# Block 2 of a Strassen-type SwiGLU kernel goes from two levels with streamed weights to one level with weights on chip, and TensorE's order is pinned

## The chip, the core and the metric

The kernel runs on one core of a Trainium2 chip. The core has TensorE (matmuls, written PE; its weight loads are listed as PEld), VectorE (DVE), ScalarE (ACT), GpSimd (POOL) and SyncE (SP), each with a queue of its own. On-chip memory is SBUF, and matmuls write to PSUM. The metric is the time of one execution on the device, in microseconds (us); less is better. All data are float32.

## The reference

The reference computes a normalised linear attention and feeds it into a gated feed-forward network:

```python
# q, k, v: (8 batches, 8 heads, 576 positions, 64)
kv = einsum('bhsd,bhse->bhde', k, v)
out = einsum('bhsd,bhde->bhse', q, kv)
out = out / sqrt(mean(out * out, axis=-1) + 1e-6) * g_norm
x = out.transpose(0, 2, 1, 3).reshape(4608, 512)      # tokens x model
g = x @ w_gate                                        # 512 x 1536
h = g * (1 / (1 + exp(-g))) * (x @ w_val)             # silu(g) * val
result = h @ w_out                                    # 1536 x 512
```

## The kernel before

**Blocks.** The 4608 tokens are cut into nine blocks of 512 (`BLK`). Each block has its attention (class `Att`), an "up" stage that makes h from x (512 to 1536 features, twice), and a "down" stage that makes the output from h. The attention of a coming block is done as a guest inside the stages of the present one: k-v products (a *visit*, line 370), scores (`heads`, line 425), squares, root, scaling, a transposition, and sums of x.

**Levels.** A product of two matrices cut into 2 x 2 quarters can be made from 7 instead of 8 products of quarters (Strassen's scheme in Winograd's form); the price is sums of quarters before and after. *One level* does this once: a unit `j` of class `Up` covers 256 features in 7 products, numbered 1, 5, 6, 2, 7, 4, 3, each of 4 matmuls with 128 x 128 weights and 256 columns (line 647). There are six units. The four base quarters of the weights lie on chip (`wg`, `wv`); three sums of them go into tiles `t`, made on GpSimd (`Up.prepare`). *Two levels* cut each of the 7 again (class `Inner`, 49 products, line 815). Its 49 weight combinations ("leaves") per unit [...]are written once to a DRAM tile `w` (`leaf_steps`, line 988) and read back in pieces of up to 256 KB into the nine `t` tiles (`Stream.pump`, lines 948 to 959).

**Schedule of blocks.** Block 0 goes up plainly, blocks 1 and 2 one after the other, blocks 3 to 8 in three pairs (class `Pair`, with `Joint`, where a matmul takes both blocks' 128 columns, 256 in all). `DEEP` = 2 is the first block with two levels. So before, block 1 is the only one that goes up by one level, and all leaves are made while it runs: from the `t` tiles for products 5, 7 and 4, and from the base quarters in place. The base quarters of the last two units are made in block 1's down stage (`latest`), and their sends are partly left to block 2's down stage (`owed_sends`). Block 2 takes 16 of its 49 leaves from the modified base quarters on chip (`RESIDENT`, `QUARTER`), the others from the stream; its matmuls have 128 columns, since it is alone.

**Memory.** The 97-KiB `arena` holds, for blocks 0 to 2, the weights (0 to 48), x (from 48), inner sums of x (from 62) and h (from 73); for the pairs, two slots each of x, inner sums and h lie over the same bytes. The ring pool `r` has 5 buffers for pieces of results and for the attention's q, squares and scaled x. PSUM pools: `b` 3 banks (the chain of products 1, 6, 7, 4 is summed on one bank and copied out by ScalarE after each), `c` 2 (products 5, 3), `a` 1 (product 2), `m` 2 (visits and scores).

**What sets the order.** The Tile framework places the instructions of all engines by priorities at build time; each engine's order is then fixed. `tc.issue_after` moves a piece behind an instruction; `in_order(engine)` chains an engine's instructions in the order of the program text, which before is used for VectorE in block 2's up stage. `fill` and `then` are dictionaries of guest work, run after a certain unit or product. `chores` (VectorE and ScalarE work) and `sends` (q loads) are lists from which each product pops one step. `ahead` (lines 1295 to 1335) gives block 2's up stage its guests: attention of block 3, of which x is turned by TensorE transposes (line 485), and k-v visits of block 4. In later blocks x is turned by VectorE in 32 x 32 tiles (`blocks_x`, line 495) and then placed by 16 DMAs (`place_x`, line 508), eight each on the queues of SP and ScalarE.

Of the kernel before, what the change touches and what calls it, by code (L numbers as in the profile page):

```python
# [14 lines left out]
P = 128  # L15
# [3 lines left out]
def kernel(  # L19
# [86 lines left out]
    KIB = 256  # L106
# [14 lines left out]
    SLOT = X + XI_  # L121
    x_slots = [x_of(span(SLOT * i, X)) for i in range(2)]
    xi_slots = [xi_of(span(SLOT * i + X, XI_)) for i in range(2)]
    h_slots = [h_of(span(2 * SLOT + H_ * i, H_)) for i in range(2)]
    both = span(0, 2 * SLOT).rearrange("p (b y) -> p b y", b=2)
    x_both = both[:, :, 0 : X * KIB].rearrange("p b (o k t) -> p b o k t", o=7, k=2)
    xi_both = both[:, :, X * KIB :].rearrange("p b (a l c) -> p b a l c", a=3, l=7)
    h_both = span(2 * SLOT, 2 * H_).rearrange("p (b f t) -> p b f t", b=2, f=NF)
# [103 lines left out]
    class Att:  # L232
# [257 lines left out]
        def blocks_x(self):  # L490


            turned = self.sq.rearrange("p f t j d -> p (f t j d)").rearrange("p (i x) -> p i x", i=2)
            for i in range(2):
                nc.vector.transpose(
                    out=turned[:, i].rearrange("p (j t c) -> p t j c", t=2, c=P),
                    in_=self.xts[:, i].rearrange("p t j u d -> p t j (u d)"),
                )
            self.turned = turned
# [122 lines left out]
    DEEP = 2  # L622
# [46 lines left out]
    class Up(Quad):  # L669
# [51 lines left out]
        def multiply(self, p):  # L721
            super().multiply(p)
            ffn = self.ffn
            if ffn.n != DEEP - 1:
                return

            if p == 5:
                self.leaf_room = ring().rearrange("p f (s c) -> p (f s) c", c=P)
            if p in (5, 7, 4):
                at = 3 * (5, 7, 4).index(p)  # L730
                ffn.making.extend(leaf_steps(self.j, [(self.w[p].unsqueeze(1), (p,))], self.leaf_room[:, at:]))
            if p == 3:
                if ffn.leaf_room is None:
                    ffn.leaf_room = xi_alone.rearrange("p a b c -> p (a b) c")
                halves = lambda t: t[self.j].rearrange("p (o i) c -> p o i c", o=2)
                steps = lambda room: leaf_steps(self.j, [(halves(wg), (1, 2)), (halves(wv), (6, 3))], room)
                if self.j < NP - 2:
                    ffn.later.extend(steps(ffn.leaf_room))
                else:
                    ffn.latest.append(steps)  # L740

    class Inner:
# [12 lines left out]
        def __init__(self, ffn, d, g, shared):  # L755
            self.ffn, self.d, self.g, self.shared = ffn, d, g, shared
            self.outers = self.GROUPS[g]
            self.ps = {}
# [27 lines left out]
        def weight(self, o, p, f):  # L786
            j = 2 * self.d + f
            if o in RESIDENT and p in QUARTER:
                w, r = {1: (wg, 0), 2: (wg, 2), 6: (wv, 0), 3: (wv, 2)}[o]
                i, e = QUARTER[p]  # L790
                return w[j][:, r + i, P * e : P * (e + 1)]
            return stream.use(self.ffn.n, self.d, o, p, f)

        def targets(self, ps, o, p):

            return [(ps[:, f], self.weight(o, p, f)) for f in range(2)]

        def operand(self, o, p):
            x = XO[o]
            if p in XI:  # L800
                return self.ffn.att.xi[:, XI[p], x]
            i, q = {1: (0, 0), 2: (1, 0), 6: (0, 1), 4: (1, 1)}[p]
            return self.ffn.att.x[:, x, i, P * q : P * (q + 1)]

        def multiply(self, p):
# [6 lines left out]
            begins = first  # L812
            for i, o in enumerate(self.outers):
                for to, weight in self.targets(ps[:, i], o, p):
                    self.ffn.multiplied = nc.tensor.matmul(  # L815
                        to, lhsT=weight, rhs=self.operand(o, p), start=begins, stop=True, skip_group_check=True,
                    )
                    begins = False
# [30 lines left out]
        def made3(self, p, e, q):  # L849
            if p != 4:  # L850
                return
            h = self.ffn.h[:, 4 * self.d : 4 * self.d + 4]
            c11, c12, c21, c22 = (self.whole(*i) for i in ((1, 1), (3, 1), (3, 0), (1, 0)))

            engine = nc.gpsimd if 4 * self.d + 4 < NF else nc.vector
            mul(engine, h[:, :, 0:HB], c11, c12)
            nc.scalar.activation(out=c21, in_=c21, func=ACT.Silu)
            mul(engine, h[:, :, HB:BLK], c21, c22)
            self.ffn.ended = self.ffn.h_sums(2 * self.d, 2, engine)

    class Joint(Inner):

        def targets(self, ps, o, p):

            return [(ps, stream.use(self.ffn.n, self.d, o, p))]

        def operand(self, o, p):  # L870
            x = XO[o]
            if p in XI:
                return xi_both[:, :, XI[p], x]
            i, q = {1: (0, 0), 2: (1, 0), 6: (0, 1), 4: (1, 1)}[p]
            return x_both[:, :, x, i, P * q : P * (q + 1)]

        def made3(self, p, e, q):
            if p != 4:
                return
            h = h_both[:, :, 2 * self.d : 2 * self.d + 2]  # L880
# [3 lines left out]
            engine = nc.gpsimd if self.d + 1 < NP else nc.vector  # L884
# [3 lines left out]
            self.ffn.ended = self.ffn.a.h_sums(self.d, 1, engine)  # L888

# [578 lines left out]
```

## Time and profile before

| | us |
|---|---|
| median of 3 runs | 1026.76 (1025.21 to 1027.19) |
| the profiled execution | 1028.97 |
| its span, first to last instruction | 1027.2 |
| start and block 0 up | 114.5 |
| block 0 down | 41.6 |
| block 1 up | 76.6 |
| block 1 down | 38.6 |
| block 2 up | 95.9 |
| block 2 down | 38.8 |
| pairs, up / down | 131 / 77, 130 / 77, 130 / 76 |

The stages are stretches of the span, cut where TensorE goes from one to the next; a few matmuls lie across each cut. A matmul of float32 shows as two records in the profile. A row of groups gives the line, engine, operation, written and read tiles, shapes and count, then busy time and the mean of one, then idle time of the engine before them with what ended it. A row of the timeline gives start, length, engine, line and operation, count, and in brackets the idle time before it. Records of the queues (PEq, SPq, ACTq) are DMA issues or the engine's own control.

### The profile page before, as it was taken

How to read it: one execution, taken by the hardware profiler on the slowest of the kernel's cores; microseconds unless marked ns; L12 is line 12 of the kernel's file. 1: busy time of each engine (PE TensorE's matmuls, PEld its weight loads, DVE VectorE, ACT ScalarE, POOL GpSimd, SP SyncE). 2: the span in 40 equal slices, each digit the busy share in tenths (PEclk: the TensorE clock that was granted, in tenths of full speed). 3: DMA queues.
4: the chain of work that ended last, by engine and by line, in shares of the span. 5: the costliest groups of instructions: out<-in, count | busy, mean ns of one | idle time of the engine just before them, and what ended most of it. 6: DMA issues, size and time to landing. Idle time of an engine off the chain costs nothing.

```text
span 1027.2 us, 17734 instructions
## 1 busy us (share of the span) xinstructions
PE 998.6 (97%) x6774; PEld 839.1 (82%) x6774; DVE 682.8 (66%) x1166; ACT 228.8 (22%) x357; POOL 359.2 (35%) x283
## 2 busy tenths in 40 slices
PE   5999999999989999999999999999999999999998
PEld 4544688888978888888888888888888888888887
DVE  2999688988557597666666755667776566666211
ACT  2765111221111211111211212211112112121100
POOL 0000263434023531444565102555651025556600
PEclk9999999999999999999999999999999999999999
DMA  7689643669788566586752364667412545543011
GB/s 219 198 266 260 122 94 129 215 212 235 230 204 223 147 201 147 164 227 157 168 149 52 101 144 149 162 169 178 120 16 67 134 144 156 161 142 101 1 41 41
DMA packets 255637, 155.20 MB, mean 151 GB/s; under 512 B 141632, under 2 KB 234816, under 8 KB 255552
## 3 DMA queue, kind: packets, MB, share of 16 engines
q1 hardware_dynamic: 215104, 148.95, 52.4%
q10 hardware_dynamic: 40384, 5.12, 3.2%
q8 instruction: 54, 0.88, 0.4%
q14 instruction: 31, 0.25, 0.1%
q0 software_dynamic: 64, 0.00, 0.0%
HBM read 117.97 MB, written 28.70 MB: 143 GB/s over the span
## 4 chain that ended last, share of the span: by engine, by line
PE 69%; DVE 3%; DMA 3%; ACTq 1%; issue 1%; ACT 0%; SPq 0%; DVEq 0%
PE b L815 24%; PE b L647 15%; PE c L815 12%; PE c L647 7%; PE a L815 6%; PE a L647 4%; DMA t<-w 3%; PE m L425 1%; PE m L370 1%; ACTq L508 1%; DVE r L132 1%; DMA ld<-in_k_dram 0%; DVE z L439 0%; DVE arena L133 0%; DVE r L134 0%
## 5 line engine op out<-in xcount | busy, mean ns | idle before, releaser
L815 PE MATMUL b<-arena,t 128*128 128x256 f32 (+1 forms) x1248 | 280.8, 363 | 7.4 <-DMA t<-w 5.3
L815 PEld LDWEIGHTS b<-arena,t 128*128 128x128 f32 x1248 | 221.2, 191 | 39.6 <-DVE r L132 5.3
L132 DVE TENSOR_TENSOR r<-b,r 128x512 f32<-128x512 f32 (+1 forms) x273 | 162.1, 606 | 94.0 <-PE b L815 85.6
L132 POOL TENSOR_TENSOR r<-r 128x256 f32<-128x256 f32 (+1 forms) x105 | 110.7, 1055 | 310.2 <-DMA t<-w 147.4
L132 DVE TENSOR_TENSOR r<-c,r 128x512 f32<-128x512 f32 (+1 forms) x179 | 108.7, 617 | 90.6 <-PE c L815 41.2
L815 PE MATMUL c<-arena,t 128*128 128x256 f32 (+1 forms) x624 | 140.8, 361 | 2.2 <-DMA t<-w 0.8
L133 POOL TENSOR_TENSOR t<-wo 128x512 f32<-128x512 f32 x54 | 76.9, 1447 | 175.8 <-DVE wo L132 105.8
L134 POOL TENSOR_TENSOR arena<-r 128x1024 f32<-128x1024 f32 (+1 forms) x46 | 96.2, 2108 | 90.8 <-DVE r L132 79.7
L815 PEld LDWEIGHTS c<-arena,t 128*128 128x128 f32 x624 | 111.1, 191 | 16.9 <-PE b L815 1.4
L132 DVE TENSOR_TENSOR r<-a,r 128x512 f32<-128x512 f32 (+1 forms) x99 | 62.4, 631 | 91.9 <-PE a L647 58.8
L133 DVE TENSOR_TENSOR arena<-arena 128x512 f32<-128x512 f32 (+3 forms) x101 | 100.5, 1007 | 18.5 <-PE b L647 11.9
L647 PE MATMUL b<-wo,arena 128*128 128x256 f32 x432 | 99.4, 382 | 0.9 <-POOL arena L134 0.8
L647 PE MATMUL b<-t,arena 128*128 128x256 f32 x432 | 96.4, 380 | 1.5 <-ACT r L1075 1.5
L647 PEld LDWEIGHTS b<-t,arena 128*128 128x128 f32 x432 | 81.8, 190 | 13.4 <-issue 2.1
L647 PEld LDWEIGHTS b<-wo,arena 128*128 128x128 f32 x432 | 80.8, 190 | 13.2 <-POOL arena L134 1.2
L829 ACT COPY r<-b 128x512 f32<-128x512 f32 x63 | 36.9, 586 | 226.1 <-PE b L815 209.3
L815 PE MATMUL a<-arena,t 128*128 128x256 f32 (+1 forms) x288 | 72.2, 366 | 0.0
L815 PEld LDWEIGHTS a<-arena,t 128*128 128x128 f32 x288 | 52.9, 190 | 6.6
L647 PE MATMUL c<-t,s 128*128 128x256 f32 x216 | 48.5, 379 | 0.0
L647 PE MATMUL a<-wo,arena 128*128 128x256 f32 x216 | 48.4, 379 | 0.0
L647 PE MATMUL c<-wo,arena 128*128 128x256 f32 x216 | 48.1, 379 | 0.0
L647 PEld LDWEIGHTS a<-wo,arena 128*128 128x128 f32 x216 | 41.0, 190 | 5.6
(118 smaller groups left out, 1115.4 us busy)
## 6 DMA issues: line engine op xcount, KB each, us to landing
t<-w SPq DMA_DIRECT2D x219, 256.0 KB, 3.1
t<-w SPq DMA_DIRECT2D x75, 128.0 KB, 3.1
out_dram<-r SPq DMA_DIRECT2D x17, 512.0 KB, 3.0
ld<-in_k_dram SPq DMA_DIRECT2D x26, 288.0 KB, 4.6
ld<-in_v_dram SPq DMA_DIRECT2D x26, 288.0 KB, 6.5
ld<-in_moe_w_gate_dram SPq DMA_DIRECT2D x12, 512.0 KB, 4.9
ld<-in_moe_w_val_dram SPq DMA_DIRECT2D x12, 512.0 KB, 4.6
ld<-in_moe_w_out_dram SPq DMA_DIRECT2D x12, 512.0 KB, 5.2
```

The costliest lines, as they stand in the source:

```text
L132: add = lambda e, o, a, b: e.tensor_tensor(out=o, in0=a, in1=b, op=OP.add)
L133: sub = lambda e, o, a, b: e.tensor_tensor(out=o, in0=a, in1=b, op=OP.subtract)
L134: mul = lambda e, o, a, b: e.tensor_tensor(out=o, in0=a, in1=b, op=OP.mult)
L370: self.positions = nc.tensor.matmul(self.kv_ps[r][u * D : (u + 1) * D, g, :], lhsT=k[:, u, c, :], rhs=v[:, u, c, :], start=(c == 0), stop= ...
L425: self.multiplied = nc.tensor.matmul(self.ps[i][u][p : p + D, t, j, :], lhsT=self.qt[rows, 2 * i + t, j, p : p + D], rhs=kvs[b % 3][rows, ...
L508: placed = queue.dma_start(out=dst[rows[b], :, rows[a]], in_=src[rows[a], :, rows[b]])
L647: self.ffn.multiplied = nc.tensor.matmul(banks[e][:, e], lhsT=lhsT, rhs=rhs, start=first and i == 0 and (e == 0 or banks[0] is not banks[1 ...
L815: self.ffn.multiplied = nc.tensor.matmul(to, lhsT=weight, rhs=self.operand(o, p), start=begins, stop=True, skip_group_check=True,)
L829: nc.scalar.copy(out=dst, in_=ps)
```

## The change

1. Block 2 goes up by one level, like block 1, from the weights on chip: `DEEP` becomes 3 (`PAIRED`), `Inner` takes over what `Joint` did, and the code for a two-level block alone, with its stream pieces (`ALONE`), goes.
2. The leaves of the base quarters are made in block 2's up stage, in place, after each unit's last product (two steps to a product); in block 1 only those of the `t` tiles are made. The last unit's are made in block 2's down stage, after product 5. No sends are owed.
3. Block 3's attention, a guest in block 2's up stage, uses ring buffers instead of homes in the arena, is turned by VectorE and placed by DMA (`turn_steps`, `place_x`, `gain_x`) instead of by TensorE transposes. Guests are placed by unit and product; each product pops up to two chores and five q loads. The q loads of blocks 3 and 4 in this stage are all issued on SP; before, SP and ScalarE shared them.
4. Block 3's inner sums run after product 7 of block 2's down stage instead of 5; block 2 needs none.
5. TensorE's order is pinned to the program's over all of block 2, and over both down stages of each pair.
6. The pairs' slots in the arena are laid out anew: two x, two inner sums, two h.

```diff
-    SLOT = X + XI_
-    x_slots = [x_of(span(SLOT * i, X)) for i in range(2)]
-    xi_slots = [xi_of(span(SLOT * i + X, XI_)) for i in range(2)]
-    h_slots = [h_of(span(2 * SLOT + H_ * i, H_)) for i in range(2)]
+    x_slots = [x_of(span(X * i, X)) for i in range(2)]
+    xi_slots = [xi_of(span(2 * X + XI_ * i, XI_)) for i in range(2)]
+    h_slots = [h_of(span(49 + H_ * i, H_)) for i in range(2)]
...
         def blocks_x(self):
+            for step in self.turn_steps():
+                step()
+
+        def turn_steps(self):
             turned = self.sq.rearrange("p f t j d -> p (f t j d)").rearrange("p (i x) -> p i x", i=2)
+            self.turned = turned
             for i in range(2):
-                nc.vector.transpose(
+                yield lambda i=i: nc.vector.transpose(
                     out=turned[:, i].rearrange("p (j t c) -> p t j c", t=2, c=P),
                     in_=self.xts[:, i].rearrange("p t j u d -> p t j (u d)"),
                 )
...
-    DEEP = 2
+    DEEP = PAIRED
...
             super().multiply(p)
             ffn = self.ffn
+            if ffn.n == 1:
+                if p == 5:
+                    self.leaf_room = ring().rearrange("p f (s c) -> p (f s) c", c=P)
+                if p in (5, 7, 4):
+                    at = 3 * (5, 7, 4).index(p)
+                    ffn.making.extend(leaf_steps(self.j, [(self.w[p].unsqueeze(1), (p,))], self.leaf_room[:, at:]))
+            if ffn.n == 2 and p == 3:
+                room = xi_alone.rearrange("p a b c -> p (a b) c")
                 halves = lambda t: t[self.j].rearrange("p (o i) c -> p o i c", o=2)
+                steps = leaf_steps(self.j, [(halves(wg), (1, 2)), (halves(wv), (6, 3))], room)
+                if self.j < NP - 1:
+                    ffn.making.extend(steps)
                 else:
-                    ffn.latest.append(steps)
+                    ffn.latest.extend(steps)
...
             for i, o in enumerate(self.outers):
-                for to, weight in self.targets(ps[:, i], o, p):
...
+                self.ffn.multiplied = nc.tensor.matmul(
+                    ps[:, i], lhsT=stream.use(self.ffn.n, self.j, o, p), rhs=self.operand(o, p),
+                    start=first and i == 0, stop=True, skip_group_check=True,
+                )
...
-            base = lambda t=t, os=os: send(os, (1, 6, 2, 3), t.rearrange("p o i e c -> p o (i e c)"))
-            if os[0] in RESIDENT and j >= NP - 2:
-                owed_sends.append(base)
-            else:
-                yield base
+            yield lambda t=t, os=os: send(os, (1, 6, 2, 3), t.rearrange("p o i e c -> p o (i e c)"))
...
-            units = []
-            for d in range(NP // 2):
-                if self.n < DEEP:
-                    units += [Up(self, 2 * d), Up(self, 2 * d + 1)]
-                else:
-                    shared = {}
-                    units += [Inner(self, d, g, shared) for g in range(4)]
+            units = [Up(self, j) for j in range(NP)]
...
-                        self.make(4)
-                        if self.chores:
-                            self.chores.pop(0)()
-                        if self.sends:
-                            self.sends.pop(0)()
+                        self.make(4 if self.n == 1 else 2)
+                        for steps, most in ((self.chores, 2), (self.sends, 5)):
+                            for _ in range(min(most, len(steps))):
+                                steps.pop(0)()
+                    fill.get((i, p) if unit is this else None, lambda: None)()
...
-                if p in (5, 7) and self.n == DEEP - 1:
+                if p == 5 and self.latest:
                     with tc.issue_after(nxt.scaled.ins), tc.issue_after(nxt.placed.ins):
-                        room = self.leaf_room if p == 5 else ring().rearrange("p f (s c) -> p (f s) c", c=P)
-                        for step in self.latest.pop(0)(room):
+                        for step in self.latest:
                             step()
...
-        def load(att, i, *pairs):
-            ffn.sends += att.quarter_steps(i, pairs, (nc.sync, nc.scalar))
+        def load(att):
+            for i in range(2):
+                ffn.sends += att.quarter_steps(i, (0, 1), (nc.sync,))
         def visits():
             visit(ffn, att, (0, 1))
-            load(att, 0, 0, 1)
-            load(att, 1, 0, 1)
+            load(att)
             then.load_kv(0)
         def turn():
             visit(ffn, then, (0,), True)
-            then.load_kv(1)
-            ffn.chores += [lambda i=i: att.turn_q(i) for i in range(2)]
+            ffn.chores += [lambda: att.turn_q(0), lambda: att.turn_q(1), lambda: then.load_kv(1)]
         def half(i):
             with tc.issue_after(ffn.multiplied.ins):
                 att.heads(i, range(NS), (m_psum, m_psum))
             ffn.visited = att.multiplied
             ffn.chores += att.chores(i)
-
-        def turn_x(i):
...
+            if i:
+                ffn.chores += att.turn_steps()
-        att.homes = {
-            "qt": h_alone[:, 8:12], "sq": span(0, 8).rearrange("p (f t) -> p f t", f=4),
-            "xts": span(8, 8).rearrange("p (f t) -> p f t", f=4),
+        return {
+            (0, 7): visits, (1, 7): turn, (2, 5): lambda: (half(0), load(then)), (3, 5): lambda: half(1), (3, 7): last,
+            (4, 5): att.place_x, (5, 1): att.gain_x, (5, 5): lambda: ffn.chores.extend(att.sum_steps()),
         }
...
-        if n:
-            ffn.down_.opens = n + 1
+        if n == 2:
+            ffn.down_.opens = PAIRED
...
-        ffn.down(nxt, {1: send, 5: inner_sums} if n == 2 else {})
+        ffn.down(nxt, {7: inner_sums} if n == 2 else {})
...
+    for n in range(PAIRED):
+        with in_order(nc.tensor.engine) if n == 2 else ExitStack():
+            alone(n)
...
-        pair.a.down(after[0] if after else None, {5: pair.second_sums})
...
-        pair.b.down(after[1] if after else None)
+        with in_order(nc.tensor.engine):
+            pair.a.down(after[0] if after else None, {5: pair.second_sums})
+            if after:
+                after[1].turn()
+            if len(after) > 2:
+                after[2].load_kv(1)
+            pair.b.down(after[1] if after else None)
```

## The prediction

> **What bounds the kernel now.** I read the page's busy times first, then busy time by stage, then TensorE's timeline in the stage that the change rewrites, then the queues of SyncE and ScalarE.
>
> ```profile
> PE 998.6 (97%) x6774; PEld 839.1 (82%) x6774; DVE 682.8 (66%) x1166; ACT 228.8 (22%) x357; POOL 359.2 (35%) x283
> ```
>
> TensorE is the bound, so time is won only where it waits or has fewer columns to do. The stages (window, its length, then busy time of PE, PEld, DVE, ACT, POOL) are block 1 up, block 1 down, block 2 up, block 2 down:
>
> ```profile
> 156.10:232.70 76.60, 76.60 (x486) 66.51 (x485) 65.80 (x134) 17.83 (x32) 30.13 (x23) 1.00 0.59 194
> 232.70:271.30 38.60, 37.84 (x293) 32.91 (x292) 27.72 (x52) 6.49 (x10) 11.36 (x8) 1.00 0.94 245
> 271.30:367.20 95.90, 86.53 (x1039) 81.29 (x1037) 61.04 (x114) 18.12 (x31) 33.92 (x26) 0.98 0.75 186
> 367.20:406.00 38.80, 37.13 (x287) 31.67 (x286) 32.23 (x44) 7.60 (x11) 9.89 (x7) 1.00 0.68 180
> ```
>
> Block 1, one level from weights on chip, needs 76.6 us; block 2, two levels and streamed, needs 95.9 us. TensorE's timeline (start, us, group) gives both paces, a streamed wait, and the pairs' start:
>
> ```profile
> 195.55 1.89 PE L647 MATMUL c<-arena 128*128 128x256 f32 x8
> 197.27 1.89 PE L647 MATMUL b<-arena 128*128 128x256 f32 x8
> ...
> 271.37 0.61 PE L815 MATMUL b<-arena 128*128 128x128 f32 x4
> 271.81 0.61 PE L815 MATMUL b<-arena,t 128*128 128x128 f32 x4
> ...
> 291.55 0.68 PE L815 MATMUL b<-arena,t 128*128 128x128 f32 x4 [1.81 <-DMA t<-w]
> ...
> 405.00 1.03 PE L815 MATMUL b<-arena,t 128*128 128x256 f32 x4
> ```
>
> A product of one level is 4 matmuls or 8 records: 1.725 us. A 128-column record takes 0.445/4 = 0.111 us. Block 2 lasts 405.00 - 271.37 = 133.6 us: 588 small records 65.4, guests in the up stage 4.7 (L370) + 2.2 (L425) + 1.9 (transposes L485), down stage 84 matmuls x 0.4314 = 36.2 and scores of block 4 2.3. That is 112.7; 20.9 us are waits and restarts, about 18 of them in the up stage.
>
> The other facts, from the timelines of SP and ACT, are that 8 q loads take 3.9 us of SP (20.3 for 32 at the worst), and that 8 placing DMAs hold ScalarE for 7.8 us, with a PSUM copy behind them:
>
> ```profile
> 100.09 20.31 SPq L333 DMA_DIRECT2D ld<-in_q_dram  x32
> ...
> 513.53 3.93 SPq L333 DMA_DIRECT2D ld<-in_q_dram  x8
> ```
>
> ```profile
> 386.03 7.76 ACTq L508 DMA_DIRECT2D arena<-r  x8
> 393.84 0.59 ACT L1075 COPY r<-b 128x512 f32<-128x512 f32 x1 [13.99 <-DMA arena<-r]
> ```
>
> [...]leaf subtractions of 128x256 average 0.618 us beside a busy GpSimd, the sums of h of that size 0.421.[...]
>
> **The change part by part.** Times U count from block 2's first product, in the instruction order of the changed program.
>
> *Products.* 42 products x 1.725 = 72.5 in place of 65.4: +7.1. The 16 TensorE transposes go: -1.9. Guests stay: L370 4.6, L425 2.2. All stream waits go: -20.9, against the new waits below. Five interruptions cost about 1.0 of restarts (block 1 up: 76.6 - 72.5 - two visits of 1.2 - 0.9 of down work begun early = 0.8 for two; both ends 0.8 to 2).
>
> *Wait A: q of block 3.* All 32 q loads now sit on SP, behind four k/v loads that wait for their buffers: 5 products 8.6 + half a visit 1.2 = U+9.8; four issues at 0.63 make 12.3. The program gives DMAs eight semaphores in turn, so each waits for the eighth before it; v lands after 6.5 us, which holds two q loads some 2.3. 32 x 0.49 + two leaf sends 1.0 + 2.3 ends at 31.4; landing 2.9 makes 34.3. VectorE, held to written order, is done with its earlier work at about 26.1, turns the first half of q and waits at the second to 34.3, then 1.2: 35.5. Behind it stand, start to start, leaf steps 0.5 + 1.0 + 0.7 + 0.5, two sums of squares 1.2, two PSUM adds 1.2, the root 2.5 (eleven small operations), two scales 1.2: 8.8, to 44.3. TensorE gets to the second half of the scores after 21 products 36.2 + visits 3.4 + first scores 1.1 = 40.7, and both "m" buffers are held until that scale. Its order is pinned, so the k-v visit, all later products and with them every PSUM copy stand behind it: A = 3.6. With q 3 us sooner 0.6; with the slow pace of 0.63 a load, 8.
>
> *Wait B.* From that scale VectorE has, in order: adds 3 x 0.6, h sums 0.7, leaf steps 2.2 + 1.0 + 0.7 + 0.5, sums of squares 1.2, root 2.5, scales 1.2, together 11.8, up to the scale of the other half. TensorE needs 1.1 + 5 x 1.725 = 9.7 to block 4's second k-v visit, which wants the same buffers: B = 2.1. If GpSimd collides less with VectorE, 0; if more, 4.
>
> *Wait C.* Block 3's x is now turned on VectorE, ready 4.7 after that scale (add 0.6, sums 0.7, leaf 1.0, two transposes 2.4), and placed by 8 DMAs on ScalarE and 8 on SP while products run. ScalarE is held 5.6 to 7.8, then Silu 0.6 and the copy that product 7 of unit 4 waits for 0.6: 11.5 to 13.7 after the scale. TensorE is there after 1.15 + 6 x 1.725 = 11.5. C = 0 to 2.2; I take 0.8. The gain by ScalarE waits for landing, with four products of slack: 0.
>
> *Leaf steps of the base blocks.* 12 a unit, 5.2 us of VectorE (2 x (0.618 + 0.577 + 0.799 + 0.618)), beside 2.9 of adds and h sums: 8.1 of a 12.1 us unit; their waits are in A to C. Block 1 is rid of them: it ran 115.3 for 113.3 of work, so 0 to -1.5; I take 0.
>
> *GpSimd.* In its new order 13 subtractions of t (1.43 each), up to unit 4's first, stand ahead of unit 0's h products, and the last two wait for TensorE to free a t tile at U+14.4 and U+16.1. So those products end at 16.1 + 2 x 1.4 + 2 x 1.4 = 21.7, before the h sums at 23.7: 0. Without that cover VectorE would stop there for some 2 us.
>
> *Down of block 2.* The last unit's leaf steps (4.6 of VectorE) and four sends (3.8 of SP) come after block 4's transposes at down+20, its placing to 27.5: sends to about 31, the first stream tiles land by 37 of 39. Hidden; uncovered 1 to 3. The placing still holds ScalarE just past product 4: 0.7 instead of 2.8. The inner sums one product later end before the pair: 0. The new buffers change addresses only: 0.
>
> *Pinned downs of the pairs.* In the first two pairs three filler matmuls go back behind, where nothing waited: 0. In the last pair the filler covers the copy between products 6 and 7:
>
> ```profile
> 961.54 5.34 PE L647 MATMUL b<-wo,arena 128*128 128x256 f32 x24
> 966.72 1.03 PE L647 MATMUL a<-wo,arena 128*128 128x256 f32 x4
> 967.61 5.42 PE L647 MATMUL b<-t,arena 128*128 128x256 f32 x24
> ```
>
> Without it TensorE waits 0.75 to 0.87, twice: +1.7.
>
> *Sum.* Block 2: 72.5 + 6.8 + 1.0 + A 3.6 + B 2.1 + C 0.8 + down 36.2 + 2.3 + 0.7 = 126.0, against 133.6: -7.6; with +1.7, -5.9. The profiled execution took 1028.97 (span 1027.2 and 1.8 around it), 2.2 above the median, so about 1023 for its like and 1026.76 - 5.9 = 1021 for the median.
>
> **Rivals.** *The whole gain comes through:* A, B and C stay small since q lands sooner or the leaf steps run at their uncontended 0.42. Then block 2 is 119 to 121 and the time about 1026.8 - 13 = 1014. For it: block 1 up ran gapless with VectorE busy 65.8 of 76.6. Against it: block 1 had no attention in that stage. *Waits change places:* A + B + C reach 12 to 14 and eat the gain, 1024.7 to 1028.8, near 1027. For it: VectorE's units 2 and 3 carry 8.1 + 5.8 us of work in 12.1. *Slower through SP's queue:* at the 0.63 a q load of the 100 us row, block 3's batch comes 4.5 later (A) and block 4's batch of 32 another 4.5, which delays the leaf sends behind it; their one staging buffer then stops VectorE before B. That is +9, so +3, 1030. It decides once the queue's delay passes 5.9 us, that is above about 0.58 a load. Against it: most rows run at 0.49.
>
> **How the numbers follow.** The measurement tells 0.2% (2.1 us) from no change. Likeliest case, 1017 to 1024.7 (point 1021): 0.50. Whole gain, below 1017: 0.22. Waits change places: 0.12. SP's queue, above 1028.8: 0.16. Faster 0.72, same 0.12, slower 0.16. The range 1013 to 1029 leaves out some 0.05 below (all waits at their lower ends and block 1 faster) and 0.15 above.
>
> **What would show it.** Right: block 2 from first product to the pairs' first in about 126 us; no L815 waits on "DMA t<-w" there; a wait of VectorE's q transpose on the q load near U+27; TensorE stopped before the second scores and the second k-v visit, by VectorE; two waits of 0.8 on ScalarE's copy in the last pair. Wrong: the up stage under 82 us or over 92, a gap before the first pair for stream tiles, or a change in the pair stages (131, 77, 130, 77, 130 us now), which I hold untouched.

## The result, and the profile after

The changed kernel takes 1033.32 us (median of 4 runs, 1031.70 to 1033.66), the kernel before, beside it, 1026.63. The ratio is 1.0064 with a 95% interval of 1.0047 to 1.0082: slower by 6.7 us, where the prediction said 5.9 us faster. The profiled execution took 1033.40, its span 1031.6.

TensorE's busy time on the page hardly moved (998.6 before), while VectorE lost 30 us of work:

```profile
PE 1000.9 (97%) x6506; PEld 835.1 (81%) x6506; DVE 653.2 (63%) x1118; ACT 232.5 (23%) x367; POOL 366.0 (35%) x290
```

The stages are the place to look. The rows are block 1 up, block 1 down, block 2 up and block 2 down; the third number from the end is the granted TensorE clock:

```profile
155.93:232.30 76.37, 76.37 (x486) 66.67 (x485) 45.21 (x105) 17.75 (x32) 28.91 (x23) 1.00 0.50 151
232.30:269.88 37.58, 37.58 (x293) 33.00 (x292) 20.55 (x32) 6.60 (x10) 22.80 (x17) 1.00 0.29 62
269.88:368.99 99.11, 86.01 (x754) 73.44 (x753) 58.75 (x105) 22.79 (x42) 30.10 (x23) 0.93 0.58 152
368.99:407.47 38.48, 38.48 (x298) 33.79 (x296) 33.85 (x52) 6.60 (x10) 10.57 (x8) 1.00 0.80 206
```

Block 1 is 1.3 us shorter (from its first product to block 2's: 113.95, before 115.21), block 2's down stage runs without a wait, and what block 2 loses against the forecast lies in its up stage: 99.1 us, where the terms of the forecast add up to 86.8. It has 13.1 us without a busy TensorE, and a granted clock of 0.93. TensorE's timeline shows both:

```profile
269.88 1.89 PE L650 MATMUL b<-arena 128*128 128x256 f32 x8
...
298.63 0.46 PE L423 MATMUL m<-kv,r 64*64 64x64 f32 x16 [0.55 <-DVE r L384]
306.50 1.56 PE L423 MATMUL m<-kv,r 64*64 64x64 f32 x48 [7.41 <-DVE r L384]
307.99 3.00 PE L650 MATMUL b<-arena,t 128*128 128x256 f32 x8
...
321.28 1.16 PE L423 MATMUL m<-kv,r 64*64 64x64 f32 x64
...
334.98 2.78 PE L368 MATMUL m<-ld 64*64 64x64 f32 x72 [3.71 <-issue]
337.69 3.50 PE L650 MATMUL b<-arena 128*128 128x256 f32 x8
...
350.11 1.97 PE L650 MATMUL b<-arena,t 128*128 128x256 f32 x8 [0.28 <-ACT r L670]
...
364.93 1.96 PE L650 MATMUL b<-arena,t 128*128 128x256 f32 x8 [0.77 <-ACT r L700]
367.15 1.99 PE L650 MATMUL c<-arena 128*128 128x256 f32 x8 [0.26 <-DVE r L130]
...
407.47 1.03 PE L801 MATMUL b<-arena,t 128*128 128x256 f32 x4
```

Two things are seen here. The stage stops twice for long: 0.55 + 7.41 us at the first scores (line 423), and 3.71 us at block 4's second k-v visit (line 368). The row names no engine for the second stop; the visit needs the two PSUM buffers "m" that VectorE's two scales of half 1 free one after the other, and VectorE does these at just that time:

```profile
334.19 1.28 DVE L132 TENSOR_TENSOR r<-m,y 128x512 f32<-128x512 f32 x2
```

What comes right after each stop is slow: a product that takes 1.89 us as listed takes 3.00 and 3.50, the scores 1.56 instead of 0.93 (as in the run with the visits first, below), the visit 2.78 instead of 1.28. That is 1.74 us after the first stop and 3.11 after the second, 4.85 in all. The granted clock of the same stretches:

```profile
305.00:310.00 5.00, 3.50 (x53) 3.02 (x54) 2.76 (x4) 1.08 (x2) 0.00 (x0) 0.50 0.86 255
...
335.00:340.00 5.00, 4.88 (x78) 4.15 (x79) 4.86 (x9) 0.39 (x2) 0.00 (x0) 0.50 0.23 82
```

It falls to 0.50. If the stop is what does this, which is tested below, a stop of TensorE is paid twice here. A stretch at 0.50 is called a dip in what follows; the two here last from 303.24 to 310.06 us and from 333.96 to 340.78.

The first stop goes back to q. VectorE's timeline has the two q transposes, SyncE's the q loads, with a leaf send left out at each row of dots:

```profile
297.25 1.24 DVE L384 STREAM_TRANSPOSE r<-ld 128x1024 f32<-128x1024 f32 x1
305.20 1.25 DVE L384 STREAM_TRANSPOSE r<-ld 128x1024 f32<-128x1024 f32 x1 [6.72 <-DMA ld<-in_q_dram]
```

```profile
283.48 11.97 SPq L331 DMA_DIRECT2D ld<-in_q_dram  x20
...
296.00 3.27 SPq L331 DMA_DIRECT2D ld<-in_q_dram  x5
...
299.79 3.59 SPq L331 DMA_DIRECT2D ld<-in_q_dram  x7
```

The 32 q loads end at 303.38, VectorE turns the second half at 305.20, and TensorE, which came to the first scores at 298.1, goes on at 306.5.

The books of the spans: start and block 0 -0.2, block 1 -1.26, block 2 +3.96 (137.59 from its first product to the pair's, before 133.63), pairs up to the last down stage 0.0, the last pair's down stages +1.9 (77.93, before 76.02). Together +4.4, the difference of the spans (1031.6 - 1027.2). The medians differ by 6.7, because the profiled execution before lay 2.3 us above its median and the one after lies on it; in which stage these 2.3 us lie, no trace shows.

### The profile page after: what moved, and what is told of

Same layout as the page of the kernel before. It is cut to its first block, busy times and chain, and to the rows that moved or that the text cites. A ratio compares the mean times of both kernels' runs of the same rounds, so it can differ in the third digit from the quotient of the medians.

```text
span 1031.6 us, 17068 instructions
## 1 busy us (share of the span) xinstructions
PE 1000.9 (97%) x6506; PEld 835.1 (81%) x6506; DVE 653.2 (63%) x1118; ACT 232.5 (23%) x367; POOL 366.0 (35%) x290
## 4 chain that ended last, share of the span: by engine, by line
PE 90%; DMA 3%; DVE 2%; SPq 2%; ACT 1%; issue 1%; POOL 1%; ACTq 0%; DVEq 0%; POOLq 0%
PE b L650 24%; PE b L801 21%; PE c L650 11%; PE c L801 11%; PE a L650 6%; PE a L801 5%; PE b L1110 4%; PE c L1110 4%; PE m L423 2%; PE m L368 1%; SPq L331 1%; DMA arena<-in_v_dram 1%; POOL t L131 1%; DMA arena<-r 1%; DMA ld<-in_v_dram 1%
## 5 line engine op out<-in xcount | busy, mean ns | idle before, releaser
L801 PE MATMUL b<-arena,t 128*128 128x256 f32 x1008 | 244.5, 381 | 0.0
L801 PEld LDWEIGHTS b<-arena,t 128*128 128x128 f32 x1008 | 190.0, 190 | 29.6 <-DVE r L130 2.4
L130 POOL TENSOR_TENSOR r<-r 128x256 f32<-128x256 f32 (+1 forms) x90 | 94.7, 1053 | 247.1 <-DMA t<-w 150.1
L130 DVE TENSOR_TENSOR r<-b,r 128x512 f32<-128x512 f32 (+1 forms) x234 | 139.0, 607 | 60.8 <-PE b L801 55.4
L132 POOL TENSOR_TENSOR arena<-r 128x1024 f32<-128x1024 f32 (+1 forms) x54 | 102.0, 1904 | 108.1 <-DVE r L130 64.2
L130 DVE TENSOR_TENSOR r<-a,r 128x512 f32<-128x512 f32 x93 | 59.3, 638 | 122.9 <-PE a L650 87.4
L801 PE MATMUL c<-arena,t 128*128 128x256 f32 x504 | 122.5, 379 | 0.8 <-ACT r L815 0.8
L801 PEld LDWEIGHTS c<-arena,t 128*128 128x128 f32 x504 | 95.6, 190 | 14.5 <-ACT r L815 1.2
L131 POOL TENSOR_TENSOR t<-arena 128x512 f32<-128x512 f32 x36 | 48.8, 1366 | 68.6 <-PE b L650 26.4
L801 PE MATMUL a<-arena,t 128*128 128x256 f32 x252 | 66.1, 379 | 0.0
```

The lines of the kernel that those rows point to most:

```text
L130: add = lambda e, o, a, b: e.tensor_tensor(out=o, in0=a, in1=b, op=OP.add)
L131: sub = lambda e, o, a, b: e.tensor_tensor(out=o, in0=a, in1=b, op=OP.subtract)
L132: mul = lambda e, o, a, b: e.tensor_tensor(out=o, in0=a, in1=b, op=OP.mult)
L801: self.ffn.multiplied = nc.tensor.matmul(ps[:, i], lhsT=stream.use(self.ffn.n, self.j, o, p), rhs=self.operand(o, p), start=first and i == ...
```

## The experiments

All are the changed kernel with the edit shown, timed beside the kernel before. "Block 2" is the time from its first product to the pair's first, from the run's trace; it is the sharper measure, since block 1 takes 113.95 or 113.96 us in all the traces of the changed kernel and its variants compared so.

| run | median, us | ratio to before (95%) | block 2, us |
|---|---|---|---|
| before | 1026.63 | 1 | 133.6 |
| after | 1033.32 | 1.0064 (1.0047 to 1.0082) | 137.6 |
| q loads on two queues | 1033.56 | 1.0055 (1.0033 to 1.0077) | 138.1 |
| visit later | 1033.76 | 1.0061 (1.0040 to 1.0082) | 138.9 |
| pairs' order free | 1030.37 | 1.0034 (1.0025 to 1.0043) | 137.3 |
| block 2's order free | 1038.94 | 1.0107 (1.0081 to 1.0134) | 145.0 |
| k-v visits first | 1023.59 | 0.9972 (0.9960 to 0.9983) | 128.2 |
| gap filled | 1031.89 | 1.0052 (1.0035 to 1.0069) | 134.5 |
| attention steps first | 1030.08 | 1.0031 (1.0019 to 1.0042) | 135.6 |
| three edits | 1018.74 | 0.9922 (0.9907 to 0.9937) | 125.7 |
| three + room in turns | 1018.66 | 0.9906 (0.9890 to 0.9922) | 125.6 |
| three + block 4's q later | 1017.92 | 0.9899 (0.9883 to 0.9916) | 124.0 |
| three + both | 1017.34 | 0.9892 (0.9874 to 0.9910) | 123.3 |

The kernel before had medians of 1026.86, 1026.39 and 1028.33 beside the three batches of experiments (the first four edits, the next four, the last three), so between batches the ratios are to be compared, not the medians.

### Undo SyncE's sole load of q

```diff
-                ffn.sends += att.quarter_steps(i, (0, 1), (nc.sync,))
+                ffn.sends += att.quarter_steps(i, (0, 1), (nc.sync, nc.scalar))
```

> The q loads of blocks 3 and 4 in block 2's up stage alternate again between SP and ScalarE; nothing else differs from the changed kernel. Theory 1 (the 32 loads on SP alone make q late, and TensorE's first scores wait for the second q transpose: 0.55 + 7.41 us, then products at a lower granted clock, some 1.7 us more): the first scores wait at most 1.5 us, the dip of the clock behind that wait goes, and the time is about 1025 (1023 to 1027). The wait at the second k-v visit (3.7 us) stays. Rival 2 (VectorE's own backlog makes the transpose late, the queue is only beside it): the wait stays above 5 us and the time within 1031 to 1034. Rival 3 (the loads hold ScalarE, whose copies are then late): the first wait goes but TensorE waits for ScalarE in units 1 and 2 instead, 1029 or more.

The time does not change. TensorE's timeline, then ScalarE's:

```profile
292.33 1.96 PE L650 MATMUL b<-arena,t 128*128 128x256 f32 x8 [1.74 <-ACT r L670]
...
303.67 0.46 PE L423 MATMUL m<-kv,r 64*64 64x64 f32 x16 [4.51 <-DVE r L384]
...
306.19 3.78 PE L650 MATMUL b<-arena,t 128*128 128x256 f32 x8
```

```profile
291.77 5.55 ACTq L331 DMA_DIRECT2D ld<-in_q_dram  x5
297.36 0.59 ACT L700 COPY r<-b 128x512 f32<-128x512 f32 x1 [5.17 <-DMA ld<-in_q_dram]
```

Theory 1 missed by over 8 us. In its numbers the result is the second case (the wait stays above 5 us, the time within 1031 to 1034), in its cause a good part of the third: five loads hold ScalarE for 5.55 us, 1.11 each, so the PSUM copies behind them are late. The copy of line 700 ends 5 us later than in the changed kernel (counted from block 2's first product), VectorE's next addition waits for it (5.63 us), and both q transposes stand behind that addition: they begin at 302.28. The wait at the first scores is still 5.1 us, and 1.74 us are lost before it. Sharing the loads again thus brings nothing back in this order of the program; what SyncE's sole load costs by itself is not shown.

### Move the second k-v visit alone

```diff
-            (0, 7): visits, (1, 7): turn, (2, 5): lambda: (half(0), load(then)), (3, 5): lambda: half(1), (3, 7): last,
-            (4, 5): att.place_x, (5, 1): att.gain_x, (5, 5): lambda: ffn.chores.extend(att.sum_steps()),
+            (0, 7): visits, (1, 7): turn, (2, 5): lambda: (half(0), load(then)), (3, 5): lambda: half(1),
+            (4, 5): lambda: (last(), att.place_x()), (5, 1): att.gain_x, (5, 5): lambda: ffn.chores.extend(att.sum_steps()),
```

> Block 4's second k-v visit moves from after product 7 of unit 3 to after product 5 of unit 4, three products later. Theory 1 (waits stand one behind the other): the 3.71 us wait before the visit goes and with it the slowed products behind it (3.1 us), but TensorE then comes 6.8 us sooner to product 7 of unit 4, whose copy stands behind the placing DMAs on ScalarE; that wait grows from 0.28 to about 6 to 7 us, and the time stays within 1030 to 1034. Rival 2 (the visit's wait alone holds the stage, ScalarE's hold is covered): the stage is 4 to 7 us shorter and the time 1026 to 1029.

As theory 1 had it, with a smaller new wait than its 6 to 7 us. The visit's wait falls to 0.5 us and its dip goes, but TensorE then meets ScalarE's hold by the placing DMAs, which the wait had covered. TensorE, then ScalarE:

```profile
348.19 3.59 PE L650 MATMUL b<-arena,t 128*128 128x256 f32 x8 [5.02 <-ACT r L670]
```

```profile
340.69 6.23 ACTq L511 DMA_DIRECT2D arena<-r  x6
...
347.47 0.58 ACT L670 COPY r<-b 128x512 f32<-128x512 f32 x1
```

The 0.28 us at this copy in the changed kernel becomes 5.02, with a dip of its own (3.59 instead of 1.89; the mean granted clock of the run is 0.993, as in the changed kernel). The waits of this stage lie one behind the other: to take this one away gained nothing (1033.76), since the next is as long.

### The pins on TensorE's order

```diff
-        with in_order(nc.tensor.engine):
+        with ExitStack():
             pair.a.down(after[0] if after else None, {5: pair.second_sums})
```

> TensorE's order is left to the scheduler again in the down stages of the pairs; block 2 stays pinned. Theory: only the last pair changes, where fillers cover the copy between products 6 and 7 again; its two waits of 0.72 and 0.68 us go, and the time is 1.4 to 1.8 us below the changed kernel, about 1031.6. Rival: the pin costs nothing there because the end of the kernel waits for the stores; no change, 1033.3.

The median is 2.9 us below the changed kernel's. The last pair's down stages take 76.2 us instead of 77.9; so 1.7 us are the pin, as the theory had it. The rest is not the edit's as far as the traces show: the one other stretch that differs by over 0.4 us ends where block 1 begins (154.54 against 155.93), ahead of all that the edit touches. The two waits of the changed kernel, and the filler in their place in this run:

```profile
970.10 2.18 PE L650 MATMUL b<-t,arena 128*128 128x256 f32 x9 [0.72 <-POOL s L130]
...
1007.27 5.45 PE L650 MATMUL b<-t,arena 128*128 128x256 f32 x24 [0.68 <-ACT r L670]
```

```profile
962.03 5.34 PE L650 MATMUL b<-wo,arena 128*128 128x256 f32 x24
967.21 1.03 PE L650 MATMUL a<-wo,arena 128*128 128x256 f32 x4
```

The other pin, over block 2, was undone in a run of its own:

```diff
-        with in_order(nc.tensor.engine) if n == 2 else ExitStack():
-            alone(n)
+        alone(n)
```

> TensorE's order is left to the scheduler in block 2; the pairs stay pinned. It then puts the first scores' larger part five products later and the second k-v visit several products later. Theory 1 (the waits come from the places at which the order is pinned): the wait at the first scores falls from 8.0 to 0 to 2 us, and the time is about 1025 (1022 to 1028), not lower because ScalarE's hold by the placing DMAs waits behind. Rival 2 (VectorE's and SP's chains set the end of the stage, whatever TensorE's order): 1031 to 1034. Rival 3 (the granted clock dips at these times by itself, whatever waits come before): the waits go, the dips to 0.5 at some 307 and 337 us of the span stay, about 1028.

All three cases missed: it is 5.6 us slower than the changed kernel. The scheduler does put products ahead of the scores, and the wait there falls to 1.39 us. But VectorE, whose order stays pinned, stops 8.90 us in front of its second q transpose, and after it has the sums, the root and the additions of several products to catch up. TensorE now runs ahead into a full PSUM bank:

```profile
318.47 2.93 PE L650 MATMUL a<-arena 128*128 128x256 f32 x6 [5.63 <-DVE r L130]
```

Later waits of 1.43, 3.71 and 2.44 us follow. The dips now begin at 316.8 and 371.4 us, with the waits of 5.63 and 3.71, and not at some 307 and 337 us, which speaks against the third case. The pin of block 2 is not the cause; with q late, it is the better of the two orders.

### Let q start sooner

```diff
-            (0, 7): visits, (1, 7): turn, ...
+            (0, 1): visits, (1, 7): turn, ...
```

Block 3's k-v visits, whose end frees the buffers for q, come after product 1 of unit 0 instead of product 7.

> Block 3's k-v visits move from after product 7 of unit 0 to after its product 1, so that the buffers for q come free 6.9 us sooner; the loads stay on SP alone. Theory 1 (q is late because its loads start late[...]; ScalarE must not carry them): q lands some 6.9 us sooner, the wait at the first scores falls from 8.0 to 0 to 1.5 us, too short to bring the granted clock down, so its 1.7 us of slowed products go too; the later waits (3.7 us and the second dip) stay. About 1024 (1022 to 1027). Rival 2 (the time comes back at the k-v visit and at ScalarE's hold, because VectorE's chain is no earlier): 1029 or more. Rival 3 (k and v of block 3 are not there yet): a new wait after product 1 of unit 0.

Theory 1 holds, and this one number turns the change from 0.64% slower to 0.28% faster. The k and v of block 3 were there, so no new wait came up. SyncE, then TensorE:

```profile
276.25 17.43 SPq L331 DMA_DIRECT2D ld<-in_q_dram  x32
```

```profile
298.58 0.46 PE L423 MATMUL m<-kv,r 64*64 64x64 f32 x16 [0.56 <-DVE r L384]
299.61 0.93 PE L423 MATMUL m<-kv,r 64*64 64x64 f32 x48 [0.57 <-DVE r L384]
...
326.45 0.33 PE L368 MATMUL m<-ld 64*64 64x64 f32 x4 [3.70 <-issue]
327.05 2.19 PE L368 MATMUL m<-ld 64*64 64x64 f32 x68 [0.27 <-DVE r L132]
```

The loads end 9.7 us sooner, 7.2 by their earlier start and 2.5 because no leaf sends stand among them and one takes 0.545 us instead of 0.59. The wait at the scores is 1.1 us, and nothing after it is slow. Block 2 is 9.35 us shorter: 6.8 of the wait, 1.7 of the first dip, 0.9 of the second, which came out shorter. The 3.70 us at the visit stay, as expected, and the rest of the visit is listed here as waiting for VectorE's scale (line 132).

### Is it the stop that slows what follows?

```diff
         def half(i):
             with tc.issue_after(ffn.multiplied.ins):
+                if i == 0:
+                    spare = m_psum.tile([P, 2, NS, D], F32, name="m").rearrange("p t j d -> p (t j d)")
+                    for _ in range(16):
+                        nc.tensor.matmul(spare[:, 0:256], lhsT=ident, rhs=ffn.att.x[:, 0, 0], start=True, stop=True)
                 att.heads(i, range(NS), (m_psum, m_psum))
```

> 16 matmuls of 128 x 256 columns, whose result nothing reads, stand ahead of the first scores and fill 6.9 us of the wait there; the wait's end is unchanged. Theory 1 (the granted clock falls because TensorE stood still[...]): no dip after the first scores, the product behind them takes 1.73 us instead of 2.84, and the stage is 1 to 2.5 us shorter there; a dip behind the later wait of 3.7 us stays. About 1031.5. Rival 2 (the dip comes from something else that happens at that time, as load on the chip): the dip stays and the time is 1033 or, with the matmuls themselves slowed, up to 1037.

The dip is gone where the gap is filled, and is still there behind the gap that is not. TensorE's timeline, then the windows with the granted clock:

```profile
298.37 7.07 PE L1229 MATMUL m<-arena,ident 128*128 128x256 f32 x32
305.37 0.58 PE L423 MATMUL m<-kv,r 64*64 64x64 f32 x16
306.34 0.93 PE L423 MATMUL m<-kv,r 64*64 64x64 f32 x48 [0.38 <-DVE r L384]
307.19 1.99 PE L650 MATMUL b<-arena,t 128*128 128x256 f32 x8
```

```profile
305.00:310.00 5.00, 4.62 (x80) 3.77 (x79) 2.83 (x4) 1.68 (x3) 0.73 (x1) 1.00 0.72 222
...
335.00:340.00 5.00, 5.00 (x30) 4.17 (x24) 4.08 (x7) 0.98 (x3) 0.00 (x0) 0.71 0.01 3
```

With seven microseconds of useless matmuls, block 2 is 3.1 us shorter. Of these only 1.6 are the filling's: the scores and the product at full pace. A q that came sooner gave 0.6, and a second dip that was shorter 0.8. The medians, 1031.89 and 1033.32, are too close for their intervals to part.

The same holds over all the traces, from some 20 us on, where their clock records begin. A single unfilled wait of TensorE between 2.79 us (room in turns) and 10.45 us (attention steps first) brought a clock of 0.50 each time. Single waits of 1.2 to 2.44 us did not: in the kernel before, the clock is 1.00 through a wait of 1.81 us that ends at 291.55. But two waits close together there, 1.26 and 0.78 us between 328.22 and 330.96, brought one dip, from 332.10 to 335.51. Where the limit lies between 2.44 us (block 2's order free) and 2.79, and whether it is a sharp one, is not shown.

The dips come in few lengths. In the clock records every dip that ends before the kernel does lasts 3.41 us (the kernel before), 6.83 (both of the changed kernel) or 10.24 (attention steps first), that is one, two or three times the same length. The same stop of 3.70 us at the visit brought 6.83 us of half clock in the changed kernel and with the pairs free, but 3.41 with two queues, with the visits first and with the gap filled. So the shorter second dip of the last two runs need not be the edit's gain; what sets a dip's length is not shown, as no run moved a stop alone. Where dips are left, one length more or less is worth about 1.7 us (an estimate, half of 3.41), and a difference of that size in block 2 between two traces need not be the edit's.

### VectorE's order

```diff
-                        self.make(4 if self.n == 1 else 2)
+                        self.make(4 if self.n == 1 else 0 if self.chores else 3)
```

> In block 2's up stage the leaf steps wait while attention steps are in the list (none to a product then, three to a product otherwise, instead of two always); the same work, in another order on VectorE. Theory 1 (leaf steps between the attention's steps make the scale of half 1, the second k-v visit and the placing late): from the first scores to the scale of half 1 VectorE needs some 20 us instead of 28, the wait at the visit (3.7 us), its dip (3.1 us) and ScalarE's hold do not come; the wait at the first scores stays. About 1026.5 (1025 to 1029). Rival 2 (VectorE waits there for TensorE and ScalarE, not for its own leaf steps): the visit's wait stays above 2.5 us, 1031 to 1034. Rival 3 (the leaf steps put off come back at the end of the stage and in the down stage): 1029 or more with a longer down stage.

Half of theory 1 came true, and the time lies above its range. The later waits go as expected: the visit waits 0.3 us, ScalarE's copy 0.5, and there is no second dip. But the wait at the first scores grew to 10.45 us:

```profile
307.48 1.25 DVE L384 STREAM_TRANSPOSE r<-ld 128x1024 f32<-128x1024 f32 x1 [10.37 <-DMA ld<-in_q_dram]
```

With three leaf steps to a product before the attention begins, four leaf sends instead of two stand among the q loads, of which the last two are issued at 303.03 to 304.94, 1.6 us later than in the changed kernel, and the transpose follows 2.3 us later. This growth was not expected; that the sends are its cause is read from the order of the queue, and was not tried apart.

### Together, and what is left

The three edits are the k-v visits first, the attention steps first, and the pairs' order free.

> Three edits together: block 3's k-v visits after product 1 of unit 0, attention steps before leaf steps, and TensorE's order left to the scheduler in the pairs' down stages. Theory 1 (the waits found are all there is): block 2 takes some 120 us from its first product to the pair's first instead of 137.6, no wait above 2 us, no dip of the clock in it; about 1015 (1013 to 1019), below the kernel before by about 1.1 per cent. Rival (another chain takes over: ScalarE's hold, the leaf sends on SP, the down stage's VectorE): 1020 or more.

The median is 8 us below the kernel before and 3.7 above the forecast. There is no wait at the scores and 0.3 us at the visit, but another chain takes over, as the rival had it, at a smaller price: a new wait at the bank of product 5, unit 5. TensorE, VectorE and SyncE:

```profile
343.03 3.40 PE L650 MATMUL c<-arena 128*128 128x256 f32 x8 [3.16 <-DVE r L130]
```

```profile
341.68 0.69 DVE L131 TENSOR_TENSOR arena<-arena 128x512 f32<-128x512 f32 x1 [3.20 <-DMA w<-arena]
```

```profile
317.63 10.99 SPq L331 DMA_DIRECT2D ld<-in_q_dram  x7
328.72 1.17 SPq L915 DMA_DIRECT2D w<-arena  x2
329.99 7.18 SPq L511 DMA_DIRECT2D arena<-r  x8
337.28 10.01 SPq L915 DMA_DIRECT2D w<-arena  x8
```

VectorE, whose next instruction is the addition that frees the bank, waits for a leaf send to leave the one staging room, and that send stands on SyncE behind block 4's q loads and the placing DMAs. Two edits tried to free it, alone and together: two places in the room for the first source (upper diff), and block 4's q loads listed after the placing (lower diff).

```diff
-                steps = leaf_steps(self.j, [(halves(wg), (1, 2)), (halves(wv), (6, 3))], room)
+                steps = [*leaf_steps(self.j, [(halves(wg), (1, 2))], room[:, 12 * (self.j % 2) :])]
+                steps += leaf_steps(self.j, [(halves(wv), (6, 3))], room[:, 6:])
```

```diff
-            (2, 5): lambda: (half(0), load(then)), ..., (4, 5): att.place_x,
+            (2, 5): lambda: half(0), ..., (4, 5): lambda: (att.place_x(), load(then)),
```

> As the three edits together, and the staging room of the base leaves is used in turns: the first source of odd units writes to a second place in it, so that VectorE need not wait for the send of the unit before. Theory 1 (the 3.16 us wait left at product 5's bank comes from VectorE, which waits for a leaf send stuck on SP behind q loads and placing DMAs): that wait falls below 1 us and the dip behind it goes; block 2 takes about 121 us instead of 125.7 and the time is about 1014.5 (1013 to 1017). Rival (SP is the bound there, the wait only moves to the next use of the room): within 1 us of 1018.7.

> As the three edits together, with block 4's q loads listed after the placing of block 3's x instead of after the first scores. Theory 1 (SP is late because of these 32 loads): leaf sends and placing run some 4 to 5 us sooner, the 3.16 us wait goes, about 1015. Rival (the loads are then late for block 4, whose q transposes stand at the start of the down stage): a wait of 2 to 6 us in the down stage, 1018 or more.

> The staging room in turns and block 4's q loads later, together. If both theories hold, no more than the better of the two alone, about 1014.5; if the late q loads cost the down stage, as that run alone.

The room alone only moved the wait, as its rival had it: 2.79 us at the last unit's product, with a granted clock of 0.50 behind it (354.26 to 357.26 us), a dip that reaches into the down stage.

```profile
352.76 2.59 PE L650 MATMUL c<-arena 128*128 128x256 f32 x8 [2.79 <-DVE r L130]
```

The later q loads did not harm block 4 (no wait in the down stage), and left 1.16, 0.77 and 1.50 us in the up stage, with the clock at 1.00 all the same; block 2 gained 1.6 us, less than the 3.7 of the forecast. Both together leave these waits. They are the best version that was run, though 2.8 us above their forecast:

```profile
335.39 1.97 PE L650 MATMUL b<-arena,t 128*128 128x256 f32 x8 [1.14 <-ACT r L670]
...
350.21 1.96 PE L650 MATMUL b<-arena,t 128*128 128x256 f32 x8 [0.77 <-ACT r L700]
...
353.05 1.99 PE L650 MATMUL c<-arena 128*128 128x256 f32 x8 [0.88 <-DVE r L130]
```

This version takes 1017.34 us, 1.1% below the kernel before. Block 2 takes 123.34; less the four waits left (3.06 with 0.27 at the visit) that is 120.3, an estimate of what one level in block 2 costs without a stall.

## Why the prediction was wrong

Its own sign of being wrong, an up stage of over 92 us, came true with 99.1.

**What was right.** One-level products take 1.725 us and nothing waits for the stream. Block 1 gave 1.26 us, inside the bound of 0 to 1.5. The down stage took 38.5 us (36.2 + 2.3 + 0.7 = 39.2 forecast), with no gap for stream tiles before the pair, and no wait of VectorE for a result of GpSimd is listed in the up stage. The pairs did not move, and the pin cost 1.9 us in the last one (1.7 forecast, 1.7 when undone). The forecast of q itself was close: VectorE waits for it for 6.72 us, and turns the second half at U+35.3 (34.3 forecast). The eight semaphores of its sum are in the changed kernel's trace: two of the q loads begin at 286.99 and 288.18, 0.02 us after block 3's v landed (286.97 and 288.16), each of which was issued eight DMAs before.

**The step that failed: Wait A.** The prediction counted the first scores as work that TensorE does when it comes to them. It let TensorE stop only at the second scores, U+40.7, for the scale that VectorE makes behind the second q transpose, and so got 3.6 us. But TensorE needs the second transpose itself, and already at the first scores, U+28. A q transpose fills two of the four head pairs for all positions (`self.qt[:, :, 2 * i : 2 * i + 2]`), while `heads(0)` takes half the positions of all four pairs. So 48 of the 64 records of the first scores, in the order of the timeline, stand behind the second transpose. The wait is 7.96 us instead of 3.6, in another place; and at the second scores, where the prediction had it, there is none. The run with the visits first shows it from the other side: with q 9.7 us sooner, this wait is 1.1 us. No run cut q and the scores along the same axis.

**The term that was missing: the clock.** The sum priced a stop at its length and about 0.2 us of restart. The two long stops cost 4.85 us more in slowed work, at a clock of 0.50; that the stop is its cause, the filled gap shows for the first of them. The profile before, too, had a dip in block 2, from 332.1 to 335.5 us.

**Wait B** was 3.71, in the bound of 0 to 4 but above the 2.1 taken. From the scale of half 0 to that of half 1 VectorE needed 14.7 us (320.80 to 335.47), not 11.8. Four of its operations there took 4.0 us longer than their like with no GpSimd operation beside them (three sums and differences of 128x256 1.31, 1.49 and 1.37 instead of 0.42, an operation of the root 1.26 instead of 0.17), and each of the four ends within 0.3 us after a GpSimd operation that ran beside it. That they waited for GpSimd fits these numbers, and so does what the prediction priced for leaf steps (0.618 us instead of 0.421), but it was not shown: no run took GpSimd's work away.

**Wait C** was 0.28 (0.8 forecast), only because B had held TensorE back; without B it is 5.02. Two waits at the end of the up stage, 0.77 and 0.26, were not in the sum.

Block 2 with the measured terms: 126.0 forecast, A +4.4, B +1.6, C -0.5, clock +4.85, end of the stage +1.0, down stage -0.7, together 136.6 against 137.6 measured. The last 1.0 was not found; restarts after the stops may be in it.

**The rivals.** *Waits change places* came nearest in size: A + B + C are 11.95, where it said 12 to 14, and it got 0.12. But its ground was VectorE's load in units 2 and 3, while the largest wait was for q, and its time of 1027 leaves out the clock. *Slower through SP's queue* named the right sign and nearly the price (18.8 us for 32 loads, 0.59 each, just over its limit of 0.58), but not the way: the loads ended only 2.1 us after the forecast, VectorE did not wait for the staging room before B, and what did the harm was that TensorE needs q earlier than the prediction had it, and the clock. That the sign fits is in this sense luck. *The whole gain* was not reached: with five edits of the order the time is 1017.34 and block 2 takes 123.3, where this rival said below 1017 and 119 to 121; the estimate of 120.3 lies in its range.

## What to carry to other kernels

When a wait is costed, look up which part of a buffer the producer fills and which the consumer reads; halves with one name can cut it along different axes, and then the first consumer waits for the last producer. In these runs a long stop of TensorE cost its length and slowed work on top: 1.74 us behind 7.96 and 3.11 behind 3.71 in the changed kernel, both at a clock of 0.50, and 1.5 behind 3.16 with three edits (3.40 instead of 1.89). Price both, and look for the wait that the stop covers before taking it away. With a pinned order, the cheapest cure here for a late load was neither another queue (1033.56) nor a free order (1038.94), but to move up the work that frees its buffer (1023.59).

## What the runs showed of the hardware that was not expected

- The granted clock fell to 0.50 at single TensorE waits of 2.79 us (room in turns) to 10.45 us (attention steps first), and each dip lasted 3.41, 6.83 or 10.24 us, so the same stop of 3.70 us cost one such length (visits first) or two (changed kernel). The matmuls put into the gap, 16 of them with a result that nothing reads, kept the clock at 1.00 from 295 to 315 us, where the changed kernel had 0.82 and 0.50 from 300 to 310, and what came behind them was 1.6 us faster.
- The 32 q loads of block 3 cost SyncE 0.545 us each (visits first) to 0.59 (changed kernel), and five in a row cost ScalarE 1.11 each in the run with two queues. There PSUM copies stood behind them, one ended 5 us late, and sharing the loads gained nothing (1033.56 us against 1033.32).
